# Query products of a row block in pairs of 64-row matmuls, and banks kept free ahead of transposes and products

## The chip, the cores and the metric

One NeuronCore of one Trainium2 chip runs the whole program. The metric is the device time of one execution in microseconds (us). TensorE (PE in the profile) multiplies, VectorE (DVE) reduces and adds, ScalarE (ACT) copies and applies functions, GpSimd (POOL) does small elementwise work and issues some DMAs, SyncE (SP) issues most DMAs. Each engine works through its own queue in order.

## The reference

Two kinds of layer alternate, each with a layer norm ahead and the input added behind: x + A(norm(x)), then x + B(norm(x)), and both once more. x has 2048 rows of 512 float32 values.

```python
def _A_ref(x, dft_seq_re, dft_seq_im, dft_hid_re, dft_hid_im):
    a = jnp.einsum("bsd,ed->bse", x, dft_hid_re)
    b = jnp.einsum("bsd,ed->bse", x, dft_hid_im)
    return jnp.einsum("ts,bse->bte", dft_seq_re, a) - jnp.einsum("ts,bse->bte", dft_seq_im, b)

def _B_ref(x, wq, wk, wv, wo):          # 32 heads of 16, one shared key and value head
    q = (x @ wq).reshape(B, S, 32, 16).transpose(0, 2, 1, 3)
    k, v = x @ wk, x @ wv
    p = softmax(einsum("bhqd,bkd->bhqk", q, k) * 16 ** -0.5)
    o = einsum("bhqk,bkd->bhqd", p, v)
    return o.transpose(0, 2, 1, 3).reshape(B, S, 512) @ wo
```

## The kernel before

The program has two layers; a layer is one A and one B. Float32 products are made of three products of rounded parts (high x high, high x low, low x high), so that `mm3` is three matmuls into one bank of PSUM.

**Phase A** runs over four row blocks `tb` of 512 rows. For each, 32 steps `n` (`n = 32 tb + 16 c + s`) accumulate the sequence transform z over the sixteen 128-row chunks `s`, for the real and the imaginary part `c`, in four banks named x. Up to step 48 the products use all 128 rows. From step 48 on `z_rows` (line 772) issues each as two products of 64 rows, one on the lower half `g = 0` and one on the upper half `g = 1`, into different banks. A group of six such pairs is followed by its counterpart in which the halves have changed banks. Since both halves then write a bank one after the other, `relay` (line 561, ACT copies one column of an operand onto itself) makes the counterpart wait until the first group is finished; another group lies in between. After both parts the y products follow (`y_tile`, or `y_rows` at line 574 on both halves), `y_out` adds the input (line 556), stores the row tile and takes its layer norm statistics (line 141, 142).

**Preparing B** for a row block happens during the next block's steps, from `base = 32 (tb + 1)`, in `prep_tasks`: layer norm (`ln_root`: an addition on DVE at line 147 and a square root on ACT; `ln_inv`: reciprocal on DVE and four operations on POOL; `ln_apply`: DVE, line 189), four transposes (`tr_tile`, line 266, into the one bank z), key and value product (`kv`, a bank y), the difference of key blocks (`k_diff`, line 304), and four query products (`q_mm`, lines 87 to 89 into a bank y, 12 matmuls of 128 rows each) at the ends of the steps `base + 7` to `base + 10`. Each is copied out of PSUM by ACT into the single tile `qraw` (line 82), rounded by ACT into its high part (83), and POOL subtracts for the low part (84). The weights of a query product come from DRAM in two loads (`wq_load`), the result goes to DRAM in six stores (`q_store`), both issued by SP. Block 0 is prepared in the steps 32 to 43, among products of 128 rows; blocks 1 and 2 among products of 64 rows. Block 3 is prepared at the end of the phase in its own way (`q_half`, `q_rows` with 256 columns at line 348, `max_two` at 405).

**Early maxima.** The softmax needs the maximum of each score row. A score product here uses only 64 rows (line 459), so single ones fit between the pairs of phase A; DVE reduces each bank (line 473, or 468 behind a Relu on ACT at 463). `EARLY` lists which query tiles may do so from which step, and by which they must be done. `pump` is called after each pair of products: it takes the entry that is due first, and `issue` picks bank z or the next of the three banks y by a table of estimated times `clk` (`spend` advances it, `held` notes until when a bank is taken). If the bank isn't free by that table nothing is issued. `flush(n)` forces what is due. Inside `q_mm` nothing is pumped.

**Phase B** then computes scores, exponentials and the products with v; the change doesn't touch it.

Lines 79 and 78 are the split of a transform chunk (POOL subtraction and ACT cast), two chunks at the start of every even step; line 759 is the copy of z out of PSUM.

Of the kernel before, what the change touches and what calls it, by code (L numbers as in the profile page):

```python
# [8 lines left out]
F32 = mybir.dt.float32  # L9
# [8 lines left out]
P = 128  # L18
S = 2048
D = 512  # L20
# [27 lines left out]
def fnet_mqa_kernel(ctx: ExitStack, tc: tile.TileContext, x_in, ct, dt_, wq, wkv, wo, out):  # L48
# [48 lines left out]
    nc.gpsimd.memset(v1[:, :, DH:DH + 1], 1.0)  # L97
    kone = sb.tile([P, 1], F32, name="kone")
# [45 lines left out]
    def ln_root(t0, n):  # L144
        v = sb.tile([P, 4], F32, name="lnv", bufs=2)[:, :n]
        w = sb.tile([P, 4], F32, name="lnw", bufs=2)[:, :n]
        nc.vector.tensor_scalar(v, mv[:, t0:t0 + n, 1], EPS, None, op0=ALU.add)
        nc.scalar.activation(w, v, AF.Sqrt)
        return t0, n, v, w
# [44 lines left out]
    def make_layer(L, src, mid, dst, last):  # L194
# [77 lines left out]

        def kv(t0, n, xth, xtl, vt=None, now=True):
            pk = bank("y")[:, :n * P]
            spend(pe=2.9, act=1.2)
            held("y", clk["pe"] + 2.5)
# [39 lines left out]
        def q_mm(tb, g, xth, xtl):  # L316
            wh, wl = st["wqh", g]
            pq = bank("y")
            spend(pe=2.9, act=1.2)
            held("y", clk["act"])  # L320
            for k in range(NK):
                ks = slice(k * P, (k + 1) * P)
                mm3(pq, wh[:, ks], wl[:, ks], xth[:, k, :], xtl[:, k, :], k == 0, k == NK - 1)
            hi = half(4 + 2 * (g % 2), F32R)
            lo = half(5 + 2 * (g % 2), F32R)
            split_act(pq, hi, lo, sb.tile([P, D], F32, name="qraw"))
            st["qs", tb, g] = hi, lo
# [104 lines left out]
        st["skew"], st["rel"], st["subs"] = 0, {}, []  # L432
# [9 lines left out]
        def issue(e, pr, part, g, force):  # L442
            i, kb = EARLY[e][:2]
            tag = "z" if clk["z"] <= clk["y"][0] else "y"
# [5 lines left out]
            if free > clk["pe"] + 0.05 and not force:  # L450
                return False
# [6 lines left out]
            pm = bank(tag)  # L458
            nc.tensor.matmul(pm, o.qT[i][gs, pr, :], k[gs, c0:c0 + 512], start=True, stop=True)  # L459
# [94 lines left out]
        def y_out(t, y, x1):  # L554
            spend(dve=1.3)
            nc.vector.tensor_add(x1, y, x1)  # L556
            nc.gpsimd.dma_start(mid[t], x1)
            ln_stats(x1, t)
# [4 lines left out]
        def y_rows(tb, pairs, zh, zl, x1, after):  # L563
            ys = [pair() for _ in pairs]
            at = 0
            for h in range(2):
                for w, y in zip(pairs, ys):
# [15 lines left out]
                    else:  # L583
                        for e in range(2):
                            y_out(4 * tb + w[e], y[:, e, :], x1[w[e]])
# [71 lines left out]
        def prep_tasks(tb, x1):  # L657
# [3 lines left out]
            def alloc():  # L661
                st["root"] = ln_root(4 * tb, 4)
# [13 lines left out]
            ts[0] = [alloc]  # L676
            ts[1, 1] = [lambda: ln_inv(*st["root"])]
# [7 lines left out]
            ts[6, 3] = [lambda: (kv_lo(4 * tb, 4), k_diff(tb) if tb < 2 else None)]  # L685
            ts[6] = [lambda: v_tr(4 * tb, 4, st["vt"])]
            for g in range(4):
                ts[7 + g] = [lambda g=g: q_mm(tb, g, *st["xt"])]
                if g < 2:
# [528 lines left out]
```

## Time and profile before

| | |
|---|---|
| median of 3 runs | 3548.38 us (3547.25 to 3548.52) |
| the profiled execution | 3548.28 us |
| its span, first to last instruction | 3546.4 us |
| PE busy | 3490.2 us, 98% of the span |
| DVE, ACT, POOL busy | 77%, 70%, 23% |
| chain of work that ended last | PE 93%, DVE 4%, ACT 2% |

In the timeline a row shows start, duration, engine, line, operation, and out<-in by the program's names; in brackets stands how long the engine was idle before it and what released it. Two products of 64 rows that start together stand in one row as x2. A product's duration includes its way through the array, so that neighbours overlap: the distance of two starts shows what a product costs.

### The profile page before, as it was taken

The numbers are of one execution on the slowest core, as the hardware profiler recorded it, in microseconds if no ns is written. First come the engines' busy times: TensorE is split into PE (matmuls) and PEld (weight loads), VectorE is DVE, ScalarE is ACT, GpSimd is POOL, SyncE is SP. The second block draws the span as 40 slices with busy tenths as digits, with TensorE's granted clock in tenths as the row PEclk, the third lists the DMA queues.
The fourth block names the chain that finished last, engine by engine and source line by source line (L and its number), as shares of the span: only waits on it lengthen the run. The fifth ranks groups of instructions, "written<-read, shape, count | busy, mean of one in ns | idle before, by whom it ended". The sixth has DMA issues, their size and how long they took to land.

```text
span 3546.4 us, 64237 instructions
## 1 busy us (share of the span) xinstructions
PE 3490.2 (98%) x24576; PEld 1884.6 (53%) x24576; DVE 2723.9 (77%) x4905; ACT 2499.3 (70%) x3204; POOL 818.7 (23%) x1212
## 2 busy tenths in 40 slices
PE   8999999999999999999999999999999999999999
PEld 6897879433333333333378978783333333333333
DVE  6267776888888888888432777768888888888883
ACT  4223733888888888888932237438888888888888
POOL 4244342211221122112213443322101110111011
PEclk9999999999999999999999999999999999999999
DMA  6445252311111100111144342423111111011100
GB/s 192 148 145 167 82 163 90 85 52 34 35 37 50 35 23 23 50 34 26 40 143 125 125 146 93 149 71 88 46 38 35 49 34 38 23 35 38 37 23 25
DMA packets 224899, 254.54 MB, mean 72 GB/s; under 512 B 52880, under 2 KB 174800, under 8 KB 217424
## 3 DMA queue, kind: packets, MB, share of 16 engines
q1 hardware_dynamic: 210384, 233.12, 21.5%
q0 software_dynamic: 14208, 17.33, 1.6%
q8 instruction: 193, 3.16, 0.4%
q14 instruction: 114, 0.93, 0.1%
HBM read 187.16 MB, written 65.27 MB: 71 GB/s over the span
## 4 chain that ended last, share of the span: by engine, by line
PE 93%; DVE 4%; ACT 2%; issue 1%; POOL 0%; DMA 0%; SPq 0%; ACTq 0%; DVEq 0%; POOLq 0%
PE z L956 29%; PE x L942 19%; PE y L398 13%; PE x L772 11%; PE y L87 3%; PE y L459 3%; PE y L88 2%; PE y L89 2%; PE x L574 2%; PE x L87 2%; PE x L89 2%; PE x L88 2%; DVE mxe L473 1%; DVE mxp L473 1%; PE z L459 1%
## 5 line engine op out<-in xcount | busy, mean ns | idle before, releaser
L945 ACT ACTIVATE slot<-x 128x1024 f32<-128x1024 f32 x2000 | 1946.2, 1024 | 284.2 <-PE x L942 272.3
L399 DVE TENSOR_REDUCE mxp<-y 128x1 f32<-128x512 f32 x2944 | 1849.8, 684 | 179.4 <-PE y L398 167.2
L956 PE MATMUL z<-slot,v 128*32 128x512 f32 x8192 | 1096.3, 605 | 1.6 <-DVE row L960 0.7
L942 PE MATMUL x<-slot,kz 64*128 64x512 f32 x2976 | 677.9, 451 | 0.7 <-DMA slot<-craw 0.4
L942 PEld LDWEIGHTS x<-slot,kz 64*128 64x128 f32 x2976 | 279.3, 184 | 742.9 <-ACT slot L945 686.4
L398 PE MATMUL y<-kz,slot 64*128 64x512 f32 x2176 | 581.2, 396 | 0.7 <-DVE mxp L399 0.4
L956 PEld LDWEIGHTS z<-slot,v 128*32 128x32 f32 x8192 | 163.4, 108 | 362.1 <-issue 331.1
L772 PE MATMUL x<-cl,xnh 64*128 64x512 f32 (+1 forms) x1536 | 352.4, 353 | 0.0
L772 PE MATMUL x<-ch,xnl 64*128 64x512 f32 (+1 forms) x1536 | 347.4, 358 | 1.1 <-ACT xnl L561 1.0
L772 PE MATMUL x<-ch,xnh 64*128 64x512 f32 (+1 forms) x1536 | 339.0, 358 | 6.5 <-DVE row L556 3.9
L398 PEld LDWEIGHTS y<-kz,slot 64*128 64x128 f32 x2176 | 277.5, 186 | 22.6 <-DVE mxp L399 10.4
L79 POOL TENSOR_TENSOR cl<-craw,ch 128x512 fp32r<-128x512 f32 x176 | 225.1, 1299 | 192.3 <-ACT ch L78 180.5
L78 ACT CAST ch<-craw 128x512 fp32r<-128x512 f32 x256 | 153.5, 622 | 156.2 <-PE x L89 81.7
L527 POOL DMA_DIRECT2D slot<-mt x224 | 111.5, 505 | 585.8 <-PE y L398 493.4
L459 PE MATMUL y<-kz,slot 64*128 64x512 f32 x602 | 232.7, 397 | 2.0 <-DVE kraw L304 1.0
L772 PEld LDWEIGHTS x<-ch,xnh 64*128 64x128 f32 x1536 | 210.0, 185 | 24.6 <-issue 6.6
L772 PEld LDWEIGHTS x<-ch,xnl 64*128 64x128 f32 x1536 | 214.3, 185 | 15.8 <-issue 4.5
L772 PEld LDWEIGHTS x<-cl,xnh 64*128 64x128 f32 x1536 | 217.3, 185 | 8.0
L997 POOL TENSOR_TENSOR row<-row,row 128x256 f32<-128x256 f32 x63 | 46.6, 739 | 700.1 <-DMA row<-rd 699.8
L473 DVE TENSOR_REDUCE mxe<-y 128x1 f32<-128x512 f32 x310 | 194.9, 680 | 14.0 <-PE y L459 14.0
L87 PE MATMUL x<-ch,xnh 128*128 128x512 f32 x384 | 154.3, 402 | 10.3 <-ACT ch L78 9.0
L89 PE MATMUL x<-ch,xnl 128*128 128x512 f32 x384 | 153.2, 399 | 2.0 <-POOL xnl L638 1.8
(197 smaller groups left out, 4173.8 us busy)
## 6 DMA issues: line engine op xcount, KB each, us to landing
craw<-ct_in SPq DMA_DIRECT2D x112, 512.0 KB
slot<-qd SPq DMA_DIRECT2D x44, 1024.0 KB
qd<-row SPq DMA_DIRECT2D x144, 128.0 KB
od<-row SPq DMA_DIRECT2D x252, 64.0 KB
row<-wqd SPq DMA_DIRECT2D x48, 256.0 KB
row<-x_in SPq DMA_DIRECT2D x32, 256.0 KB
mid<-row POOLq DMA_DIRECT2D x32, 256.0 KB, 2.4
craw<-ct_in SPq DMA_DIRECT2D x32, 256.0 KB
```

Of the source, the lines that this page charges most:

```text
L78: nc.scalar.copy(hi, raw)
L79: (eng or nc.vector).tensor_sub(lo, raw, f(hi))
L87: nc.tensor.matmul(ps_, ah, bh, start=start, stop=False)
L89: nc.tensor.matmul(ps_, al, bh, start=False, stop=stop)
L398: nc.tensor.matmul(pm, o.qT[i][gs, pr, :], kz[gs, c0:c0 + n], start=True, stop=True)
L399: nc.vector.reduce_max(to, pm, axis=AX.X)
L459: nc.tensor.matmul(pm, o.qT[i][gs, pr, :], k[gs, c0:c0 + 512], start=True, stop=True)
L473: nc.vector.reduce_max(to, pm, axis=AX.X)
L772: nc.tensor.matmul(z[d], a[gs, s, d * P:(d + 1) * P], b[gs, :], start=first and q < 2 and e == 0, stop=last and q > 1 and e == len(turns) - 1)
L942: nc.tensor.matmul(st["e"][:, g, :], kz[64 * g:64 * g + KR, c * P:(c + 1) * P], o.qT[i][64 * g:64 * g + KR, cp:cp + 4, :], start=True, sto ...
L945: nc.scalar.activation(ptiles[i, s_][:, 2 * w:2 * w + 2, :], st.pop("e"), AF.Exp, scale=DH ** -0.5)
L956: nc.tensor.matmul(a[32 * j:32 * j + 32, :], v1[:, c, :], pt[:, j, :], start=c == 0, stop=c == NT - 1)
```

## The change

The query products of a row block are made two at a time in `q_pair`: each of the 24 weight and activation pairings becomes two 64-row matmuls, one on each row half, for two query groups in two banks y; in the second half of the 48 the halves change banks, with a `relay` in between. After every two matmuls `pump` is called. `keep_two` takes the two banks at `(base + 7, 1)` and `(base + 9, 1)`, that is after the second quarter of a step; until the pair is issued only one further use of a bank y is allowed, and bank z. The pairs stand at the ends of the steps `base + 7` and `base + 9`.

`keep` takes a bank y ahead of the key product in the same way. `hold` closes bank z to maxima ahead of each transpose and of the value transposes. The steps of the preparation move forward by up to one step; layer norm goes by two tiles at a time, its addition moves from DVE to POOL, and the square root adds epsilon itself. In `y_rows` both additions come ahead of both statistics. Four of the eight last maxima move from the second `q_rows` to the second half of the first. Starts in `EARLY` move by up to one step.

```diff
-    (1, 0, 2, 44, 49, 63, 16), (2, 0, 3, 44, 49, 63, 16), (3, 0, 8, 45, 49.5, 66, 16), (0, 0, 0, 64, 66.5, 79, 16),
-    (0, 1, 0, None, 71.5, 79, 16), (3, 1, 8, None, 71.5, 84, 16), (4, "f", 2, 77, 79.5, 95, 16), (5, "f", 3, 77, 79.5, 95, 16),
+    (1, 0, 2, 43, 48, 63, 16), (2, 0, 3, 43, 48, 63, 16), (3, 0, 8, 44, 48, 66, 16), (0, 0, 0, 64, 66.5, 79, 16),
+    (0, 1, 0, None, 70.8, 79, 16), (3, 1, 8, None, 70.8, 84, 16), (4, "f", 2, 76, 78.5, 95, 16), (5, "f", 3, 76, 78.5, 95, 16),
...
-        nc.vector.tensor_scalar(v, mv[:, t0:t0 + n, 1], EPS, None, op0=ALU.add)
-        nc.scalar.activation(w, v, AF.Sqrt)
+        nc.scalar.activation(w, mv[:, t0:t0 + n, 1], AF.Sqrt, bias=eps)
+        nc.gpsimd.tensor_scalar(v, mv[:, t0:t0 + n, 1], EPS, None, op0=ALU.add)
...
+        def keep(after):
+            st["pk"], st["kept"] = bank("y"), 3
+            held("y", clk["pe"] + 1.4 + 2.8 + after)
...
+        def keep_two():
+            st["pqs"], st["kept"] = [bank("y"), bank("y")], 2
+            for e in range(2):
+                held("y", clk["pe"] + 1.4 + 5.8 + 0.8 * e)
+
+        def q_pair(tb, g0, xth, xtl, n):
+            pq = st["pqs"]
+            for h in range(2):
+                for k in range(NK)[::1 - 2 * h]:
+                    ks = slice(k * P, (k + 1) * P)
+                    for u in (0, 1, 2)[::1 - 2 * h]:
+                        for g in order(0, 1):
+                            gs = slice(64 * g, 64 * g + 64)
+                            wh, wl = st["wqh", g0 + (g ^ h)]
+                            a, b = ((wh, xth), (wh, xtl), (wl, xth))[u]
+                            nc.tensor.matmul(pq[g ^ h], a[gs, ks], b[gs, k, :],
+                                             start=(h, k, u) == (0, 0, 0), stop=(h, k, u) == (1, 0, 0))
+                        spend(pe=0.231)
+                        pump(n)
+                if h == 0:
+                    relay(xth[:, NK - 1, :1])
+                    pump(n)
+            st["kept"] = 0
+            spend(act=2.4)
+            raw = sb.tile([P, D], F32, name="qraw")
+            for e in range(2):
+                hi, lo = half(4 + 2 * e, F32R), half(5 + 2 * e, F32R)
+                split_act(pq[e], hi, lo, raw if e == 0 else sb.tile([P, D], F32, name="qraw"))
+                st["qs", tb, g0 + e] = hi, lo
...
-            tag = "z" if clk["z"] <= clk["y"][0] else "y"
+            tag = "z" if clk["z"] <= clk["y"][0] and not st["hold"] else "y"
...
+            if tag == "y" and st.get("kept") == 1:
+                return False
...
                         for e in range(2):
-                            y_out(4 * tb + w[e], y[:, e, :], x1[w[e]])
+                            y_add(4 * tb + w[e], y[:, e, :], x1[w[e]])
+                        for e in range(2):
+                            ln_stats(x1[w[e]], 4 * tb + w[e])
...
-            ts[2, 0], ts[2, 2] = [ap(0)], [ap(1)]
-            ts[2] = [lambda: tr(0)]
-            ts[3, 0], ts[3, 2] = [ap(2)], [ap(3)]
-            ts[3] = [lambda: tr(1)]
-            ts[4, 1] = [lambda: tr(2)]
-            ts[4] = [lambda: tr(3), lambda: [wq_load(g) for g in range(2)]]
-            ts[6, 0] = [do_kv]
...
+            ts[0, 0] = [alloc, lambda: root_(0)]
+            ts[0, 2] = [lambda: ln_inv(*roots[0])]
+            ts[1, 1] = [ap(0), lambda: root_(2)]
+            ts[1, 2] = [ap(1), hold]
+            ts[1, 3] = [lambda: ln_inv(*roots[2])]
+            ts[2, 0] = [lambda: tr_(0)]
+            ts[2, 1] = [hold]
+            ts[2, 2] = [ap(2)]
+            ts[2, 3] = [ap(3), lambda: tr_(1)]
+            ts[3, 0] = [hold]
+            ts[3, 1] = [lambda: tr_(2)]
+            ts[3, 2] = [hold]
+            ts[4, 0] = [lambda: tr_(3), lambda: [wq_load(g) for g in range(2)]]
+            ts[4, 3] = [lambda: keep(2.6)]
+            ts[5, 1] = [do_kv]
+            ts[6, 0] = [lambda: (kv_lo(4 * tb, 4), k_diff(tb) if tb < 2 else None), hold]
+            ts[6, 2] = [lambda: (st.update(hold=False), v_tr(4 * tb, 4, st["vt"]))]
+            for e in range(2):
+                ts[7 + 2 * e, 1] = [keep_two]
+                ts[7 + 2 * e] = [lambda e=e: q_pair(tb, 2 * e, *st["xt"], base + 8 + 2 * e)]
+            ts[7].append(lambda: [wq_load(g) for g in (2, 3)])
+            ts[8] = [lambda: [q_store(tb, g) for g in (0, 1)]]
+            ts[10] = [lambda: [q_store(tb, g) for g in (2, 3)]]
...
-            q_rows(14, 0, *xt[1], lambda: None)
+            ticks = iter([0, 0, 0, 0, 1, 1, 1, 1])
+            q_rows(14, 0, *xt[1], lambda: take(mb, next(ticks)))
```

## Rows read from the trace of the kernel before

**Rows 1.** The page, part 2: granted TensorE clock in 40 equal slices, in tenths.

```profile
PEclk9999999999999999999999999999999999999999
```

**Rows 2.** Busy time by stretch: length, then each engine's us (and count).

```profile
136.00:176.00 40.00, 40.00 (x185) 32.35 (x184) 6.38 (x7) 15.48 (x28) 15.78 (x12) 1.00 0.53 157
```

**Rows 3.** Table of waits: who waited for whom, total us, times, longest us.

```profile
PE z L266 <- DVE mxp L473: 7.0, 6, 2.3
PE z L266 <- DVE mxe L473: 5.3, 6, 1.4
PE x L772 <- DVE row L556: 3.9, 4, 1.0
PE y L87 <- DVE mxe L473: 2.8, 6, 0.5
PE y L87 <- DVE mxp L473: 1.9, 4, 0.5
PE y L459 <- DVE kraw L304: 1.0, 2, 0.5
...
ACT lnw L148 <- POOL lnw L157: 11.9, 5, 2.4
```

**Rows 4.** Timeline of PE at three query products of block 1, first layer.

```profile
310.89 0.39 PE L89 MATMUL y<-slot,row 128*128 128x512 f32 x1
311.21 0.51 PE L772 MATMUL x<-ch,xnh 64*128 64x512 f32 x2
311.54 0.39 PE L459 MATMUL y<-kz,slot 64*128 64x512 f32 x1
...
314.79 0.45 PE L772 MATMUL x<-ch,xnl 64*128 64x512 f32 x2
315.17 0.50 PE L87 MATMUL y<-slot,row 128*128 128x512 f32 x1
315.51 0.39 PE L88 MATMUL y<-slot,row 128*128 128x512 f32 x1
...
322.61 0.50 PE L87 MATMUL y<-slot,row 128*128 128x512 f32 x1 [0.46 <-DVE mxp L473]
```

**Rows 5.** Timeline of PE at the turn inside block 3's first query pair.

```profile
621.74 0.28 PE L348 MATMUL x<-xnh,cl 64*128 64x256 f32 x2
622.30 0.38 PE L348 MATMUL x<-xnh,cl 64*128 64x256 f32 x2 [0.28 <-ACT xnh L561]
```

**Rows 6.** Timeline of ACT, then POOL, behind the query product that ends at 311.

```profile
311.31 0.60 ACT L82 ACTIVATE qraw<-y 128x512 f32<-128x512 f32 x1 [5.66 <-PE y L89]
311.94 0.62 ACT L83 CAST row<-qraw 128x512 fp32r<-128x512 f32 x1
312.47 1.14 ACT L78 CAST ch<-craw 128x512 fp32r<-128x512 f32 x2
...
312.72 1.29 POOL L84 TENSOR_TENSOR row<-qraw,row 128x512 fp32r<-128x512 f32 x1 [13.07 <-PE y L459]
```

**Rows 7.** Timeline of PE, then DVE, behind the last y products of block 1.

```profile
270.70 0.50 PE L772 MATMUL x<-ch,xnh 64*128 64x512 f32 x2 [1.01 <-DVE row L556]
...
269.12 0.70 DVE L141 BATCH_NORM_STATS2 bst<-row 128x6 f32<-128x512 f32 x1
```

**Rows 8.** Timeline of POOL and DVE in the layer norm of block 1.

```profile
271.50 2.54 POOL L79 TENSOR_TENSOR cl<-craw,ch 128x512 fp32r<-128x512 f32 x2
271.63 2.45 DVE L147 TENSOR_SCALAR lnv<-mv 128x4 f32<-128x4 f32 x1
```

**Rows 9.** Timeline of PE, then DVE, at the end of the first phase A.

```profile
630.92 0.27 PE L533 MATMUL y<-ident,ms 128*32 128x128 f32 x1 [2.06 <-DVE ms L516]
...
625.16 4.93 DVE L407 TENSOR_REDUCE mxp<-y 128x2 f32<-128x512 f32 x8 [2.86 <-PE y L405]
```

**Rows 10.** Timeline of PE at forced maxima, first layer: first and last row.

```profile
407.97 0.40 PE L459 MATMUL y<-kz,slot 64*128 64x512 f32 x1
...
410.95 0.50 PE L459 MATMUL y<-kz,slot 64*128 64x512 f32 x1 [0.20 <-ACT rel L463]
```

More of the change, by code (lines that the diff above doesn't have):

```diff
@@ L97, in fnet_mqa_kernel @@
     nc.gpsimd.memset(v1[:, :, DH:DH + 1], 1.0)
+    eps = sb.tile([P, 1], F32, name="eps")
+    nc.gpsimd.memset(eps, EPS)
     kone = sb.tile([P, 1], F32, name="kone")
@@ L271, in tr_tile, with kept @@
                 split_ps(v[0], xth, xtl)
+        def keep(after):
+            st["pk"], st["kept"] = bank("y"), 3
+            held("y", clk["pe"] + 1.4 + 2.8 + after)
+        def kept():
+            st["kept"] = 0
+            return st["pk"]
         def kv(t0, n, xth, xtl, vt=None, now=True):
-            pk = bank("y")[:, :n * P]
+            pk = (bank("y") if now else kept())[:, :n * P]
             spend(pe=2.9, act=1.2)
-            held("y", clk["pe"] + 2.5)
+            if now:
+                held("y", clk["pe"] + 2.5)
             for k in range(NK):
@@ L314, in v_tr @@
             nc.scalar.copy(v1[:, t0:t0 + n, :DH], pv_[:, :, DH:])
[L316 to L327, printed above, removed]
+        def keep_two():
[19 more added lines that the diff above has]
+                    pump(n)
+            st["kept"] = 0
+            spend(act=2.4)
[4 more added lines that the diff above has]
+                st["qs", tb, g0 + e] = hi, lo
         def q_half(t0, g, xth, xtl, between=lambda: None):
@@ L431, in make_layer @@
                 for e, ent in enumerate(EARLY)}
-        st["skew"], st["rel"], st["subs"] = 0, {}, []
+        st["skew"], st["rel"], st["subs"], st["hold"] = 0, {}, [], False
+        roots = {}
         def pump(n, only=None):
@@ L458, in issue @@
             pm = bank(tag)
+            if tag == "y" and st.get("kept"):
+                st["kept"] -= 1
+                assert st["kept"]
             nc.tensor.matmul(pm, o.qT[i][gs, pr, :], k[gs, c0:c0 + 512], start=True, stop=True)
@@ L554, in y_out, with y_add @@
         def y_out(t, y, x1):
-            spend(dve=1.3)
+            y_add(t, y, x1)
+            ln_stats(x1, t)
+        def y_add(t, y, x1):
+            spend(dve=1.5)
             nc.vector.tensor_add(x1, y, x1)
             nc.gpsimd.dma_start(mid[t], x1)
-            ln_stats(x1, t)
         def relay(ap):
@@ L661, in alloc @@
             def alloc():
-                st["root"] = ln_root(4 * tb, 4)
                 st["xt"] = [slot(2 + j, F32R).rearrange("p (k t) -> p k t", k=NK) for j in range(2)]
@@ L674, in ap @@
                 return lambda: (spend(dve=0.8), ln_apply(x1[j], x1[j], 4 * tb + j))
-            ts[0] = [alloc]
-            ts[1, 1] = [lambda: ln_inv(*st["root"])]
-            ts[2, 0], ts[2, 2] = [ap(0)], [ap(1)]
-            ts[2] = [lambda: tr(0)]
-            ts[3, 0], ts[3, 2] = [ap(2)], [ap(3)]
-            ts[3] = [lambda: tr(1)]
-            ts[4, 1] = [lambda: tr(2)]
-            ts[4] = [lambda: tr(3), lambda: [wq_load(g) for g in range(2)]]
-            ts[6, 0] = [do_kv]
-            ts[6, 3] = [lambda: (kv_lo(4 * tb, 4), k_diff(tb) if tb < 2 else None)]
@@ L686, in prep_tasks, with hold, tr_ @@
[L686 to L689, printed above, removed]
-                    ts[7 + g].append(lambda g=g: wq_load(g + 2))
-                if g:
-                    ts[7 + g].append(lambda g=g: q_store(tb, g - 1))
-            ts[11] = [lambda: q_store(tb, 3)]
+            def hold():
+                st["hold"] = True
+            def tr_(tt):
+                st["hold"] = False
+                tr(tt)
@@ new lines, in root_ @@
+            def root_(e):
+                roots[e] = ln_root(4 * tb + e, 2)
+            ts[0, 0] = [alloc, lambda: root_(0)]
[8 more added lines that the diff above has]
+            ts[3, 0] = [hold]
```

4 rows, old and new, of the table EARLY are left out of this document.

## The prediction, made before the changed kernel ran

> **What bounds the kernel now.** The profiled execution took 3548.28 us around a span of 3546.4 us; that is 0.1 us from the median of the three runs, so a change of the span is taken as a change of the time. The page comes first: TensorE (PE) is busy nearly throughout, and its clock is granted in full (2.4 GHz) in every slice [rows 1]. So nothing is gained off PE, and a microsecond counts only if PE's stream of products gets shorter or loses a gap. "Busy" hides small gaps, because products overlap: two 64-row products, one on each row half, start together and last 0.39 us, while the next two start 0.23 us later. The second view is therefore PE's own table of waits, which says where its stream stands still and for whom [rows 3]; the third is the timeline of single stretches, read by the distance of starts against that pitch of 0.23 us. The phases with the sequence transform (about 0 to 632 and 1772 to 2394 us) hold everything that the change touches. In them the preparation of row block 0 runs among 128-row products: 136 to 176 us are 40.00 us busy of 40.00 [rows 2], there is nothing to gain there. Blocks 1 and 2 are prepared among 64-row products with single row maxima ("maxima" below: one 64-row product of 512 columns, then a DVE reduction that frees its bank) between them, and there the waits lie.
>
> **What the change takes away** (both layers together, four preparations of blocks 1 and 2):
>
> *Turns between 64 and 128 rows.* Each of the 16 query products is a run of 12 full products among 64-row ones. Going in, the starts lie 0.38 us apart instead of 0.23 (0.15 lost), going out 0.32 and then 0.33 (0.09 and 0.10) [rows 4]; the second pitch inside is 0.34 (0.11). That is 0.45 us a product, 16 x 0.45 = 7.2 us. As pairs of 64-row products they take the same pitch as their neighbours, and this goes. The Trainium skill says so too (TensorEngine Tiling (Array Packing), Key Properties: changing the tiling mode, not just the tile, drains the engine); by it alone the turn would go as well, so the sum is the same.
>
> *Waits of query products for a bank.* 2.8 + 1.9 us in ten waits [rows 3], such as 0.46 us at 322.61 [rows 4]. With two banks set aside half a step ahead they go: 4.7 us, and 0.07 us each for refilling the pipe, 5.4 us.
>
> *Waits of transposes.* 7.0 + 5.3 us in twelve waits [rows 3]: the one z bank is held by a maximum whose reduction stands in DVE's queue. Closing z ahead of each transpose takes that away. But the transposes now come up to three quarters of a step earlier (a step is 2.8 us of products), and the first of a block then waits for its normalised rows. That chain stands behind two subtractions on POOL, 2.54 us together, in POOL's queue ahead of the new addition [rows 8]; they start when the y additions are out, some 0.7 us earlier than now. By my estimate its end and the due time of the transpose fall together, with no slack. In return DVE loses an operation that took 2.45 us beside POOL's subtractions, for 4 columns [rows 8]. I take 10.5 us of the 12.3; bounds 6 and 12.3.
>
> *The y additions first.* After the last y products PE waits for the addition that frees its bank, 3.9 us in four waits [rows 3], 270.70 one of them; the statistics that now go behind (0.70 us, and a short aggregate) stood between the two additions [rows 7]. 3.3 us.
>
> *The wait for the K difference.* 1.0 us in two waits [rows 3], with refilling and the maxima behind it about 2.8; the bank is now counted as taken 2.6 us longer and the subtraction starts half a step earlier. I take half, 1.4; bounds 0 and 2.8.
>
> *End of the phase.* PE waits 2.06 us for the last maxima, whose eight reductions run from 625.16 for 4.93 us, 0.616 each [rows 9]. Four of them may start behind the first query pair, about 2 us earlier. The last then ends near 628.0 instead of 630.1, about when PE has finished its products, so nearly the whole wait goes: 1.8 us a layer, 3.6.
>
> *Maxima forced at their due time.* Between 407.97 and 410.95 eight single products start and nothing else, where 0.12 us each would do: 2.0 us a layer [rows 10]. The pairs now let about five maxima through where a query product let none, and starts move up by up to a step, so fewer are left. I take 2.5 us of 4.0; bounds 0 and 4.0.
>
> Together 12.6 + 10.5 + 3.3 + 1.4 + 3.6 + 2.5 = **33.9 us**.
>
> **What the change adds.**
>
> *A turn inside each pair.* Both row halves write both banks, so the second half of a pair starts only when the first half is finished and ACT has copied one column onto itself. The same sequence stands at the end of the phase with 256 columns: starts 621.74 and 622.30, 0.56 us where 0.12 (half of 0.23) would do, 0.44 lost [rows 5]. The 128-row form needs no such turn. A single maximum (0.12) may fill part of it: 0.35 us, eight pairs, 2.8 us; bounds 1.6 and 3.6. The Trainium skill speaks against the change here (TensorEngine Tiling (Array Packing), Gotcha 1: different row tiles cannot access the same PSUM bank simultaneously); it gives no price, so the sum stays with the row.
>
> *Behind each pair: ACT and POOL.* This is the term that decides. A query product leaves ACT two copies, 0.60 and 0.62 us, the first starting 0.42 us after the start of its last product (310.89), then POOL a subtraction of 1.29 us from 312.72 [rows 4, 6]. Until now the next came a step and a product later. Now two results are finished at once, and both go through the one tile `qraw`. The second copy out of PSUM has to wait until POOL has read the first. That a copy waits for POOL to release a reused tile is in the trace (ACT's Sqrt behind POOL, 11.9 us in five waits) [rows 3]. Counted from the start of the pair's last product: first bank free at 1.02, second copy of it to 1.67, POOL 1.83 to 3.12, second bank free at 3.8, last copy to 4.45. The planner counts them free 7.2 and 8.0 us after they are set aside, and itself counts 6.9 us of products and some 0.7 of maxima from there to the pair's end. So it sends the next maximum into the first bank at 0.47 (PE waits to 1.07: 0.6) and, one or two pitches later, another into the second bank at 1.85 (PE waits to 3.85: 2.0). PE's queue is in order, so the transform's products stand behind that. 2.6 us a pair, eight pairs: 20.8 us. Were no maximum to go there, PE would still need ACT's one-column copy of the next step, behind two casts of 0.57 us [rows 6]: ready about 5.9, needed about 3.7, 2.2 us. Bounds: 0.6 a pair (4.8), if the second copy doesn't wait, and 3.2 (25.6).
>
> *Block 0.* Its products run without a gap [rows 2]; two pairs a layer now put a turn in and out (0.45) and one inside (0.44) there, with no maxima to fill it: 4 x 0.89 = 3.6 us. Behind the second pair POOL reaches the low part of a transform chunk only after both query subtractions, at about 7.2, and PE needs it at 6.2: 1.0 us a layer. 5.6 us; bounds 2 and 7.
>
> Weights: the second pair's four loads (1 MB) start behind the first pair with two steps and its stalls to land, 8 us and more; counted at nothing, and 1 us a pair if that cover falls short. The stores on SP are the same in number; they wait for the same copies.
>
> Together 2.8 + 20.8 + 5.6 = **29.2 us**. Net 4.7 us shorter: 3548.3 - 4.7 = **3543.6 us**. The time is a small difference of two large terms.
>
> **Rivals.**
>
> *The copies behind a pair cost little.* If the maxima find other banks until the second copy is out, or `qraw` isn't waited for, 0.6 us a pair stays: 16 us less, 3527.6, own range 3519 to 3536. For it: z and the third bank are free then, and PE's waits named in the table are short. Against it: the planner's own figures make both banks free at once.
>
> *The transposes wait for POOL instead of DVE; slower.* The new addition and the normalising chain stand on POOL behind two subtractions of 1.27 us [rows 8], with no slack by the sum above. If they come 2 us later, each block's first transpose waits over 2 us again, the scaling holds up DVE's reductions behind it, and so the next transposes: the 10.5 us are lost and about 1.5 us a block added. 3543.6 + 10.5 + 6 = 3560. It decides from a delay of about 2 us on. Against it: the additions come earlier, and the chunk subtractions may start earlier with them.
>
> *The halves don't run together.* A pair needs two weight loads. If they went one after the other, the pitch would be near 0.37 and each pair 3.4 us longer, 12 pairs, 3584 us. The Trainium skill has loads cost by their columns, not by their rows (TensorE: Matmul & The Clock Gate, LDWEIGHTS), which alone would ask for that. The neighbours in the same form keep 0.23, so this has hardly a chance.
>
> **How the numbers follow.** Forecast 0.48 (own range 3537 to 3551), cheap copies 0.33, POOL slower 0.17, halves 0.02. A measurement of this kernel tells about 0.2%, 7 us, from no change. Faster by more (under 3541.3): all of the second case and a quarter of the forecast, 0.45. Slower by more: most of the third and the last, 0.16. Within: 0.39. The range 3524 to 3553 takes in the second case's centre and the forecast with its bounds; it leaves out the third case and the far end of the second.
>
> **What would show it.** Right: no gap ahead of transposes in blocks 1 and 2 beyond the turn's 0.2 us; query pairs at a pitch of 0.23 with one gap near 0.45 in the middle; behind each pair ACT's second copy starting at the end of POOL's subtraction, with PE waiting for it near 2 us. Wrong: PE running on behind a pair (second case), or transposes waiting for the scaling behind POOL (third).

## The result, and the profile after

The changed kernel takes 3555.13 us in the median (3551.99 to 3558.51), the kernel before 3550.38 (3547.25 to 3552.29): a ratio of 1.0014, 95% interval 1.0008 to 1.002. It is 4.75 us slower where 4.7 us were to be gained, and lies above the range. The profiled execution has a span of 3552.1 us, 5.7 more than before's.

The table shows where the 5.7 us arise. It takes the start of each step's transform products in both timelines, less the pitch of the products between them; what is left is how far one kernel falls behind the other, step by step. Each timeline is one execution, with the clock falls of that one.

| part of the change | forecast, us | measured, us |
|---|---|---|
| y additions first | -3.3 | -4.2 |
| transposes | -10.5 | -8.8 |
| **K difference: steps of the key product and the value transposes** | **-1.4** | **+8.5** |
| query products of blocks 1 and 2 (-12.6 + 2.8 + 20.8) | +11.0 | +8.1 |
| block 0 | +5.6 | +5.3 |
| end of the phase | -3.6 | -2.8 |
| forced maxima | -2.5 | -0.9 |
| the rest | 0 | +0.5 |
| sum | -4.7 | +5.7 |

PE's table of waits in the changed kernel (waiting engine, tile and line <- releaser: us in total, times, longest) answers [rows 3]:

```profile
PE y L493 <- ACT qraw L82: 6.7, 8, 1.2
PE z L268 <- DVE row L191: 3.5, 3, 2.2
PE y L342 <- ACT slot L598: 3.4, 12, 0.3
PE y L493 <- DVE kraw L315: 2.5, 2, 1.3
PE x L88 <- POOL cl L79: 1.5, 2, 0.8
PE y L493 <- DVE kz L305: 1.1, 2, 0.6
```

The twelve waits of transposes for reductions and the four for y additions are gone. In their place stand eight waits for `qraw`, one for each pair of blocks 1 and 2; twelve turns inside pairs; one long wait of a transpose, now for the scaled row (the other two of the three stood before as well, at block 3); two late chunks in block 0; and the wait for the K difference, which was 1.0 us and is now 2.5, with 1.1 for the subtraction ahead of it.

**The K difference.** The timelines of DVE and PE in the changed kernel, block 1 of the first layer (start, us, engine, line, operation, out <- in, count, [idle before <- releaser]):

```profile
300.27 0.69 DVE L507 TENSOR_REDUCE mxp<-y 128x1 f32<-128x512 f32 x1 [0.26 <-PE x L825]
301.00 1.39 DVE L305 TENSOR_TENSOR kz<-y,kz 16x512 fp32r<-16x512 f32 x2
302.40 0.69 DVE L315 TENSOR_TENSOR kraw<-kraw,y 128x512 f32<-128x512 f32 x1
...
303.24 0.46 PE L493 MATMUL y<-kz,slot 64*128 64x512 f32 x1 [1.27 <-DVE kraw L315]
```

A single maximum has been sent into the bank of the key product, and waits until DVE has read it. DVE does that in 0.69 us, but first it reduces a fourth maximum (300.27) and makes the two subtractions of `kz`. Before, three maxima stood ahead of them and PE waited 0.50 us. What follows costs more than the wait. PE's busy time and granted clock by stretch, in the changed kernel and then in the kernel before (stretch, its length, busy (count), granted clock, DMA share, GB/s):

```profile
305.00:306.00 1.00, 1.00 (x8) 0.67 0.00 0
306.00:307.00 1.00, 1.00 (x8) 0.50 0.00 0
307.00:308.00 1.00, 1.00 (x8) 0.50 0.00 0
308.00:309.00 1.00, 1.00 (x8) 0.63 0.00 0
...
2067.00:2069.00 2.00, 2.00 (x11) 0.50 0.00 0
```

```profile
305.00:306.00 1.00, 0.74 (x5) 1.00 0.00 0
306.00:307.00 1.00, 1.00 (x12) 1.00 0.00 0
```

Behind the wait TensorE's clock falls from 2.4 to 1.2 GHz. The four stretches of 1 us hold 0.66 + 1 + 1 + 0.74 = 3.4 us at half clock with PE busy throughout: 1.7 us lost. In the second layer it is twice that, 6.8 us and 3.4 lost. Waits of 3.6 us instead of 1.0 and 5.1 us of half clock make 7.7 of the 8.5; the rest is put down to the refilling of the pipe and was not measured apart. PE shows as 1.00 busy in all of it; the clock column tells, and the count beside it (8 products started in a microsecond instead of 12). The page's row of clocks is all nines here as in [rows 1], since a slice of 89 us hides such a stretch.

**Behind a query pair.** ACT, POOL and PE in the changed kernel, first pair of block 1:

```profile
317.10 0.60 ACT L82 ACTIVATE qraw<-y 128x512 f32<-128x512 f32 x1 [3.39 <-PE y L342]
319.81 0.60 ACT L82 ACTIVATE qraw<-y 128x512 f32<-128x512 f32 x1 [1.46 <-POOL row L84]
...
318.51 1.27 POOL L84 TENSOR_TENSOR row<-qraw,row 128x512 fp32r<-128x512 f32 x1 [15.38 <-PE x L825]
...
313.76 1.45 PE L342 MATMUL y<-slot,row 64*128 64x512 f32 x10 [0.28 <-ACT slot L598]
320.46 0.49 PE L493 MATMUL y<-kz,slot 64*128 64x512 f32 x1 [1.18 <-ACT qraw L82]
```

This is as forecast, down to the place: the second copy starts at 319.81, when POOL's subtraction ends (318.51 + 1.27 = 319.78), and a maximum in the second bank holds PE until it is out. PE stands still for 1.18 us there, not 2.0. The turn inside the pair is the 0.28 at 313.76, 0.45 to 0.52 us by the distance of starts.

**The end of the phase.** DVE's last reductions and PE's outer products behind them, changed kernel:

```profile
627.57 4.92 DVE L435 TENSOR_REDUCE mxp<-y 128x2 f32<-128x512 f32 x8 [0.89 <-PE y L433]
...
633.34 0.27 PE L567 MATMUL y<-ident,ms 128*32 128x128 f32 x1
634.82 0.50 PE L426 MATMUL y<-kz,slot 64*128 64x512 f32 x1 [0.78 <-DVE mxp L427]
```

The eight reductions start 0.89 us behind DVE's last work instead of 2.86, and the wait of 2.06 us of [rows 9] is gone; 0.78 us of it comes back at the next maxima.

**The forced maxima.** They are forced at two places. PE at the first of them, changed kernel, first and last row:

```profile
413.04 0.50 PE L493 MATMUL z<-kz,slot 64*128 64x512 f32 x1
...
416.58 0.49 PE L493 MATMUL y<-kz,slot 64*128 64x512 f32 x1 [0.19 <-ACT rel L497]
```

From 413.04 up to 416.58 nine single products start and nothing else, in 3.54 us, where [rows 10] has eight in 2.98 us. Here none has gone. The second place, which [rows 10] does not show, is the next due time; in the kernel before, first and last row:

```profile
554.10 0.40 PE L459 MATMUL y<-kz,slot 64*128 64x512 f32 x1
...
555.29 0.50 PE L459 MATMUL y<-kz,slot 64*128 64x512 f32 x1 [0.18 <-DVE mxe L468]
```

Five single products start there and nothing else, in 1.19 us (and at 2316.06 in the second layer). In the changed kernel no such row of maxima is left at that place, and the two steps around it are 1.35 and 1.15 us shorter in the two layers. The first place costs 1.6 us more than before, the second 2.5 less.

### The profile page after: what moved, and what is told of

It is laid out like the page before. It is cut to its first block, busy times and chain, and to the rows that moved or that the text cites. A ratio compares the mean times of both kernels' runs of the same rounds, so it can differ in the third digit from the quotient of the medians.

```text
span 3552.1 us, 64858 instructions
## 1 busy us (share of the span) xinstructions
PE 3502.6 (99%) x24864; PEld 1872.6 (53%) x24864; DVE 2720.8 (77%) x4892; ACT 2504.3 (71%) x3222; POOL 830.9 (23%) x1262
## 5 line engine op out<-in xcount | busy, mean ns | idle before, releaser
L426 PE MATMUL y<-kz,slot 64*128 64x512 f32 x2176 | 581.8, 396 | 1.9 <-DVE mxp L427 1.9
L825 PE MATMUL x<-ch,xnh 64*128 64x512 f32 (+1 forms) x1536 | 347.7, 359 | 2.3 <-ACT row L812 2.2
L493 PE MATMUL y<-kz,slot 64*128 64x512 f32 x622 | 247.5, 405 | 12.2 <-ACT qraw L82 6.7
L825 PEld LDWEIGHTS x<-ch,xnl 64*128 64x128 f32 x1536 | 205.8, 185 | 18.7 <-ACT xnl L598 3.8
```

The costliest lines, as they stand in the source:

```text
L426: nc.tensor.matmul(pm, o.qT[i][gs, pr, :], kz[gs, c0:c0 + n], start=True, stop=True)
L825: nc.tensor.matmul(z[d], a[gs, s, d * P:(d + 1) * P], b[gs, :], start=first and q < 2 and e == 0, stop=last and q > 1 and e == len(turns) - 1)
```

## Experiments

Times are medians; each ratio is to the kernel before, run on the same chip (3550.5 to 3550.9 us). "Changed kernel" is the kernel after, 3555.1. A profile is one execution of several, and where its clock falls differs between executions; readings by steps come from that one.

**1. The second copy of a pair in a tile of its own.** Everything else as in the changed kernel.

```
-            raw = sb.tile([P, D], F32, name="qraw")
...
-                split_act(pq[e], hi, lo, raw if e == 0 else sb.tile([P, D], F32, name="qraw"))
+                split_act(pq[e], hi, lo, f(lo))
```

> The changed kernel, but the second copy out of PSUM no longer shares the tile qraw: ACT copies each result into the tile of its low part, and POOL subtracts there in place. Theory (ACT waits for POOL behind each pair, and PE for ACT): in the profile ACT's second copy starts right behind its first cast instead of 2.7 us after the first copy; PE's waits for ACT's copies behind pairs (6.7 us in eight in the changed kernel) fall to under 2, and the time by 5 to 8 us against the changed kernel, to about that of the kernel before. Rival (the maxima in between hide it, PE's waits only move to the next bank): under 2 us.

Measured: 3545.66 us, ratio 0.9985 (0.9976 to 0.9994), 9.5 below the changed kernel. ACT in this run, behind the same pair:

```profile
318.42 0.60 ACT L82 ACTIVATE row<-y 128x512 f32<-128x512 f32 x1 [3.37 <-PE y L342]
...
319.58 0.59 ACT L82 ACTIVATE row<-y 128x512 f32<-128x512 f32 x1
```

The second copy starts 1.16 us behind the first, instead of 2.71, and waits for nothing; the eight waits for `qraw` are out of PE's table. Step by step each pair of blocks 1 and 2 is 1.05 to 1.52 us shorter, 10.3 together, and the late chunk of block 0 goes too (about 1.9 us). So the one tile `qraw` is the cause of the waits behind pairs, and 10.3 us its price in blocks 1 and 2. Clock falls at other places (285.7 and 415.4 us are two) take some of it back.

**2. Single 128-row query products again,** in all blocks and at their old steps, with the rest of the change kept (the first maxima of block 0 then start at their old times too).

```
-            for e in range(2):
-                ts[7 + 2 * e, 1] = [keep_two]
-                ts[7 + 2 * e] = [lambda e=e: q_pair(tb, 2 * e, *st["xt"], base + 8 + 2 * e)]
+            for g in range(4):
+                ts[7 + g] = [lambda g=g: q_mm(tb, g, *st["xt"])]
...
```

> The changed kernel with the four query products of 128 rows of before in all blocks, at the old steps; all else as changed. Counted along the steps of the two profiles, pairs cost about 2 us more than single products in each of the blocks 1 and 2 (8 us) and 2.6 us in block 0 (5 us). Theory: 11 to 14 us faster than the changed kernel, 6 to 9 us faster than before. Rival (the losses stand in the steps of the key product and not in the pairs): 4 us or less from the changed kernel.

Measured: 3543.24 us, ratio 0.9982 (0.9973 to 0.9991), 11.9 below the changed kernel. The query steps of blocks 1 and 2 are 10.8 us shorter, block 0 4.5. Part of it comes back: 3.1 us at the first forced maxima, with clock falls, and 3.7 at the end of the phase, where the second row of forced maxima stands again. In blocks 1 and 2 that is what the pairs reach too once their copies don't wait (10.3). A pair saves the turns between 64 and 128 rows, and loses about as much by its own turn in the middle (0.45 to 0.52 us) and by the maximum that meets its first bank (0.2 to 0.4).

**3. Single query products in block 0 alone.** The same edit under `if tb == 0`.

> The changed kernel with the single query products of before in block 0 alone. Theory (two turns of row mode, two turns inside and one late chunk in each layer): 5 us faster than the changed kernel, half of it in each layer, all between the steps 39 and 46. Rival (block 0 has cover): nothing.

Measured: 3549.66 us, ratio 0.9999 (0.999 to 1.0008), 5.5 below the changed kernel, against the 5.6 us of the sum and the 5.3 of the traces.

**4. The bank of the key product counted as taken 2 us longer.**

```
-            ts[4, 3] = [lambda: keep(2.6)]
+            ts[4, 3] = [lambda: keep(4.6)]
```

> The changed kernel with one number changed: the planner counts the bank of the key product as taken 2.0 us longer (4.6 instead of 2.6). No maximum is then sent between the key product and the value transposes into that bank. Theory (PE's wait of 1.3 us for the key difference in block 1, and the clock at 1.2 GHz behind it for 3.4 and 6.8 us): both are gone from block 1, in both layers, and the time falls by 5 to 8 us. Rival A (the clock falls there without the wait): the stretches near 305 and 2064 us stay, and 2 to 3 us are gained. Rival B (the maxima held back wait elsewhere): under 1 us.

Measured: 3549.19 us, ratio 0.9997 (0.9988 to 1.0006), 5.9 below the changed kernel. PE's stretches in this run:

```profile
305.00:306.00 1.00, 0.98 (x8) 1.00 0.86 262
306.00:307.00 1.00, 0.85 (x8) 1.00 0.01 0
307.00:308.00 1.00, 1.00 (x9) 1.00 0.00 0
```

No maximum meets the bank, the wait for `kraw` is out of the table, and the clock stays at 2.4 GHz where it fell. So the changed kernel counted the bank free too early. In this profile the steps of the K difference are 6.1 us shorter than in the changed kernel, of the 8.5; some comes back as a wait of the transform for the copy of the values (1.8 us in two). The profile is of the longest of the eleven executions, 3555.48 us: its clock falls for 3.4 us at five other places between the products, behind transposes, query pairs and forced maxima (286.3 and 416.0 us are two), where the profile of the changed kernel has none. How many such falls the median execution has is not on record.

**5. The same wait, put into the kernel before.** Two additions of 0.69 us on DVE, whose results are overwritten, ahead of the K difference of block 1.

```
             t = st["kraw"]
+            for _ in range(2):
+                nc.vector.tensor_add(kd, t, t)
```

> The kernel before with two more DVE additions of 512 columns (0.69 us each, into a tile that is written over afterwards) ahead of the key difference of block 1. It doubles one wait of before. Theory (a wait long enough lets the clock fall): PE's wait for the key difference grows from 0.5 to near 1.9 us, a stretch at half clock follows within some microseconds in one layer or both, and the time grows by 1.4 us a layer for the wait and 1.7 or 3.4 us a layer for the clock: 5 to 9 us. Rival (only the wait counts): 2 to 3 us, the clock stays full.

Measured: 3555.99 us, ratio 1.0015 (1.0006 to 1.0024), 5.5 above the kernel before. PE's wait and PE's stretches in this run:

```profile
306.24 0.50 PE L461 MATMUL y<-kz,slot 64*128 64x512 f32 x1 [1.96 <-DVE kraw L306]
...
307.00:308.00 1.00, 0.77 (x6) 0.91 0.00 0
308.00:309.00 1.00, 1.00 (x6) 0.50 0.00 0
309.00:310.00 1.00, 1.00 (x8) 0.50 0.00 0
```

The wait grows from 0.50 to 1.96 us, and the clock falls behind it, with nothing of the change in the kernel. Step by step each layer loses 2.7 us there, for a wait that is 1.4 us longer. In the second layer the clock falls behind the same wait (1.96 us at 2071.30, fall at 2072.51). All eleven executions took longer than any of the kernel before, so this is not one unlucky profile. That a wait of this kind brings the clock down here is thereby shown; that every such wait does is not (see the last section).

**6. Key product, K difference and value transposes at their old steps,** no bank set aside for them, and the start times of the maxima of the keys as before (71.5 and 103.5 instead of 70.8 and 102.8).

```
-            if now:
-                held("y", clk["pe"] + 2.5)
+            held("y", clk["pe"] + 2.5)
...
-            ts[4, 3] = [lambda: keep(2.6)]
-            ts[5, 1] = [do_kv]
-            ts[6, 0] = [lambda: (kv_lo(4 * tb, 4), k_diff(tb) if tb < 2 else None), hold]
-            ts[6, 2] = [lambda: (st.update(hold=False), v_tr(4 * tb, 4, st["vt"]))]
+            ts[6, 0] = [do_kv]
+            ts[6, 3] = [lambda: (kv_lo(4 * tb, 4), k_diff(tb) if tb < 2 else None)]
+            ts[6] = [lambda: v_tr(4 * tb, 4, st["vt"])]
...
```

> The changed kernel with the key product, the key difference and the value transposes at the steps of before, no bank set aside for them and z open to maxima there. Theory (in the changed kernel PE waits 1.3 us for the bank of the key difference, and TensorE's clock falls to 1.2 GHz for 3.4 and 6.8 us behind that wait): the wait falls to 0.5 us, no stretch at half clock is left in block 1, and the time falls by 6 to 9 us. Rival A (the move itself costs, not the clock): full clock only changes 0 to 2 us. Rival B (the clock falls whatever stands there): the half-clock stretches stay, at other places.

Measured: 3563.16 us, ratio 1.0037 (1.0024 to 1.0049), 8.0 above the changed kernel. PE's table of waits in this run has new lines:

```profile
PE z L492 <- ACT v L324: 4.2, 2, 2.1
PE z L268 <- DVE mxp L506: 3.8, 2, 1.9
```

The K steps of block 1 are 1.85 and 3.0 us shorter, and the clock no longer falls there in the first layer; in the second it falls for 3.4 us instead of 6.8, behind a new wait of 2.10 us (2075.15, for the copy of the values). A wait as long, for the same copy, stands in the first layer (309.29) and leaves the clock as it is. The maxima, moved with them, now meet the value transposes and block 3. The undo moved more than the suspect and decides nothing about it; experiments 4 and 5 do.

**7. Another form of the scaling.** Rows of blocks 0 to 2 scaled by `scalar_tensor_tensor` instead of `tensor_scalar`.

> The changed kernel, with the scaling of the normalised rows in blocks 0 to 2 as a two-tensor operation on DVE (the factor broadcast along the row) instead of a tensor-scalar operation. Theory (a tensor-scalar operation on DVE stands still while POOL runs its subtractions: 4.12 us at 281.5 beside 5.0 us of POOL): all these scalings take near 0.7 us, the wait of 2.2 us of the third transpose in block 1 goes, and the time falls by 2 to 5 us. Rival (the operation waits for its operands, the row shows the wait): its duration stays near 4 us, the time the same.

Measured: 3558.71 us, ratio 1.0024 (1.0014 to 1.0033), 3.6 above the changed kernel. The third scaling of block 1 on DVE, and POOL beside it:

```profile
282.75 4.59 DVE L715 SCALAR_TENSOR_TENSOR row<-row,mv,rs 128x512 f32<-128x512 f32 x1
287.86 0.74 DVE L715 SCALAR_TENSOR_TENSOR row<-row,mv,rs 128x512 f32<-128x512 f32 x1
...
281.81 2.54 POOL L79 TENSOR_TENSOR cl<-craw,ch 128x512 fp32r<-128x512 f32 x2
284.30 2.48 POOL L84 TENSOR_TENSOR slot<-row,slot 128x512 fp32r<-128x512 f32 x2
```

The other form stands still here beside POOL just as the first does (4.12 us in the changed kernel), and costs 0.74 instead of 0.53 where it is free.

**8. The scaling ahead of POOL.** The third and fourth scaling issued behind the first transpose.

```
-            ts[2, 0] = [lambda: tr_(0)]
+            ts[2, 0] = [lambda: tr_(0), ap(2), ap(3)]
```

> The changed kernel, with the third and fourth scaling of rows in blocks 0 to 2 (tensor_scalar on VectorE) issued three quarters of a step earlier, behind the first transpose. Theory: in the changed kernel the third scaling of block 1 takes 4.12 us at 281.51 instead of 0.5, because it starts while GpSimd runs its four subtractions of 280.37 to 285.34, and ends with them; the third transpose waits 2.19 us for it. Its mean and root are there at 279.25, ahead of GpSimd's subtractions and of VectorE's reductions. Issued there it takes 0.5 us a piece, the table's waits of transposes for scaled rows (3.5 us in three) go, and the time falls by 3.5 to 5 us, to 3550 to 3552. Rival: the operation waits for its rows or their root and not for GpSimd; then the waits stay within 1 us of 3.5 in sum, or go to the second transpose, and the time stays at 3555.

Measured: 3562.88 us, ratio 1.0042 (1.0028 to 1.0057), 7.8 above the changed kernel. DVE, POOL, and PE's table in this run:

```profile
280.08 0.55 DVE L191 TENSOR_SCALAR row<-row,mv,rs 128x512 f32<-128x512 f32 x1 [1.15 <-POOL rs L160]
280.54 4.73 DVE L191 TENSOR_SCALAR row<-row,mv,rs 128x512 f32<-128x512 f32 x1
...
281.26 2.50 POOL L79 TENSOR_TENSOR cl<-craw,ch 128x512 fp32r<-128x512 f32 x2
283.72 1.25 POOL L84 TENSOR_TENSOR slot<-row,slot 128x512 fp32r<-128x512 f32 x1
...
PE y L493 <- DVE mxp L507: 5.8, 2, 4.0
```

The root came out at 280.05, as POOL's last step ahead of its subtractions. One scaling passed in 0.55 us; the next was caught and ended at 285.27, 0.30 behind POOL's three subtractions. It had begun 0.72 us before the first of them (281.26), while POOL was issuing transfers (280.06, for 1.19 us). Four reductions now stood behind it, and PE waited 4.0 us for one of them. The remedy failed, and it shows that not one scaling's place in the program makes it slow: now another one is, beside the same row of subtractions.

**9. Two parts of the change alone,** in the kernel before: the y additions ahead of the statistics, and four of the last eight maxima taken behind the first pair.

> The kernel before with two parts of the change alone: the y additions ahead of the statistics, and four of the last eight maxima of the phase taken behind the first pair of its last query products. Theory (the parts add up as the step by step comparison of the two traces has them): -4.15 us for the additions and -3.6 to -5.3 for the end of the phase, 3550.5 - 7.8 to 9.5 = 3541 to 3543. Rival: the gain at the end comes from the changed spread of maxima over the blocks and not from the four taken early; then only the additions are left, 3546.

Measured: 3544.81 us, ratio 0.9983 (0.9974 to 0.9993), 6.1 below the kernel before, between the two theories. The trace has the parts as they were in the whole: 3.9 us for the additions, and the wait for the last maxima 2.0 us a layer shorter. What takes some of it back is the clock behind a transpose of block 1: it waits 2.26 us for its bank at 279.97, as it did before at 280.92 with the clock at 1.00, and now the clock falls behind it (at 280.60 and 2041.88; 1.6 us in each layer by the steps). Two waits of 0.8 us at block 3 are new. The transpose in this run:

```profile
279.97 0.66 PE L266 MATMUL z<-ident,row 128*128 128x128 f32 x4 [2.26 <-DVE mxp L473]
```

**10. The mended parts together.** The copy of its own, the bank taken 2 us longer and single products in block 0; first with the other scaling of experiment 7, then without it, then with the scaling of experiment 8.

> The changed kernel with four edits together: single query products in block 0, the low part's tile in place of qraw in the pairs, the longer count for the key product's bank, the scaling as a two-tensor operation. If the gains add up (9.5 and 5 us as measured one by one, 5 to 8 and 2 to 5 as expected for the other two): 20 to 25 us faster than the changed kernel, 16 to 20 us faster than before. If the clock falls at other places instead, half of that.

Measured: 3536.93 us, ratio 0.9959 (0.9947 to 0.9972).

> The changed kernel with three edits: the bank of the key product counted as taken 2.0 us longer, the second copy of a query pair into the tile of its own low part, and block 0 with single 128-row query products. It is the best version so far without the other form of the scaling, which by itself cost 3.6 us. Theory that the parts add up: 3555.1 - 5.9 - 9.5 - 5.5 = 3534.2, some 3533 to 3537 (the in-place copy is worth less where block 0 has no pairs). Rival: the clock falls to 1.2 GHz at other waits as one is taken away, 3537 to 3541.

Measured: 3531.24 us, ratio **0.9948** (0.9934 to 0.9963), 19.7 below the kernel before and 23.9 below the changed one. PE's stretches in this run:

```profile
271.00:300.00 29.00, 26.73 (x203) 1.00 0.48 158
300.00:400.00 100.00, 98.13 (x820) 1.00 0.51 156
400.00:620.00 220.00, 216.37 (x2092) 1.00 0.35 110
2000.00:2365.00 365.00, 359.47 (x3234) 1.00 0.37 117
```

The parts add up and 3 us more: 5.9 + 9.5 + 5.5 = 20.9. The clock stays at 2.4 GHz from 271 to 620 and from 2000 to 2365 us; it falls only at the ends of the phases, as in the kernel before. The run with the other form of the scaling is 5.7 us longer. That this is the form's own price is not shown: its profile has four clock falls of 3.4 us that this one lacks (19.5, 285.7, 412.0 and 2166.5 us), 6.8 us together.

> The version before this one with the third and fourth scaling issued earlier, behind the first transpose. Theory: 3.5 to 5 us less than it, about 3530. Rival, as for the scaling alone: no change.

Measured: 3539.45 us, ratio 0.9971 (0.9961 to 0.9982): 8.2 us above the kernel without the earlier scaling, with a wait of 4.1 us and two clock falls in its profile (281.5 and 2039.4 us).

## Why the prediction was wrong

**The step that failed is "the wait for the K difference".** The text took half of 2.8 us as a gain, because the bank "is now counted as taken 2.6 us longer and the subtraction starts half a step earlier", and set the lower bound at nothing. It measured 8.5 us the other way, which is 9.9 of the 10.4 us between forecast and profile.

The ground of the gain was not there. The kernel before, too, counted the bank as taken behind the product: `kv` advances the planner's time by its product and then calls `held("y", clk["pe"] + 2.5)`. `keep(2.6)` adds 1.4 for the half step up to the product, 2.8 for the product, and 2.6. Counted from the end of the product, the planner takes the bank as occupied for 2.6 us instead of 2.5: 0.1 us longer, not 2.6. Nor does an earlier subtraction help, since the product moves with it: three quarters of a step lie between the two in both kernels. So nothing in the change could shorten the wait. Experiment 4 gives the bank the 2 us that the text thought it had, and the wait goes.

Two things made it longer. What stands ahead of the subtraction on DVE was not counted in the new order: a fourth reduction besides the subtractions of `kz`, so that the bank comes free at 303.09 (302.40 + 0.69), 5.65 us after the key product's last product has ended (297.05 + 0.39), against 4.70 before. And no row of a stretch behind a wait was read for its clock. The waits cost 2.6 us more than before, the clock 5.1 us. Experiment 4 takes both away, experiment 5 makes both in the kernel before.

**Forced maxima** came out at -0.9 for -2.5, inside the bounds, but not where the text looked. At the place of [rows 10] it lost 1.6 us: 302 maxima have started ahead of that step; before, 304 had. The 2.5 us came at the next due time, which the text didn't count: by then 533 have started, and before 527. That part is due to the pairs, as forecast: in experiment 1, which has them, the second row of forced maxima is gone, and in experiments 2 and 9, with single products, it stands. Experiment 2 has the moved starts of the changed kernel, so these alone don't take it away. That the sum of the two falls inside the bounds is luck.

**Behind each pair** the mechanism was right in each link (one `qraw`, ACT held by POOL, a maximum in the second bank holding PE), and experiment 1 shows it by taking the tile away. The size was not: 10.3 us for the second copies, where 2.0 us of each 2.6 were to be theirs, 16 us. In the pair shown, the maximum that met the second bank stood waiting from 319.28, 2.2 us behind the start of the first copy, where the text had it at 1.4 (1.85 less 0.42). The query steps as a whole came out at +8.1 instead of +11.0.

**Transposes:** 8.8 us of the forecast 10.5, inside the bounds. In blocks 1 and 2 the waits for reductions went altogether. One long wait is left, for the third scaling of block 1 in the first layer:

```profile
279.71 1.89 DVE L507 TENSOR_REDUCE mxp<-y 128x1 f32<-128x512 f32 x3 [1.58 <-PE y L493]
281.51 4.12 DVE L191 TENSOR_SCALAR row<-row,mv,rs 128x512 f32<-128x512 f32 x1
286.16 0.53 DVE L191 TENSOR_SCALAR row<-row,mv,rs 128x512 f32<-128x512 f32 x1
...
280.37 2.54 POOL L79 TENSOR_TENSOR cl<-craw,ch 128x512 fp32r<-128x512 f32 x2
...
285.78 0.63 PE L268 MATMUL z<-ident,row 128*128 128x128 f32 x4 [2.19 <-DVE row L191]
```

So the second rival had its place right, POOL's subtractions beside the normalising, and its reason half: not POOL's own chain is late, but one of DVE's scalings stands still beside POOL. [Rows 8] had shown the like, an operation on 4 columns that took 2.45 us beside the same subtractions; the sum used it as a gain and not as a price for what stands there next. In the second layer the same scaling passed in 0.54 us (last section).

**The rest held.** y additions -4.2 for -3.3, block 0 +5.3 for +5.6 (experiment 3: 5.5, with the late chunk as forecast, 0.76 us of wait at 181.14), the turn inside a pair 0.45 to 0.52 us for 0.35, and the end of the phase -2.8 for -3.6. There the reductions start 2.0 us earlier, as forecast, the wait of 2.06 us goes and 0.78 comes back; the clock behind it in the first layer was low for 6.8 us and not for 10.2. The rival of cheap copies did not come: the second copy waits in each of the eight pairs. Its 16 us were 9.5 us of time when experiment 1 made the copies cheap.

The net was a small difference of two large terms, and the text says so; yet its range allowed 9 us upwards, and the one term of the K difference, whose lower bound was set at nothing, came out 9.9 us above its forecast. The other terms are off by less than 3 us each and together by 0.5.

## What to carry to other kernels

Before a reservation is priced as longer than the one it replaces, both are counted from the same event: here 2.6 us were 0.1. And the account of when a PSUM bank comes free goes through the queue of the engine that reads it, in the new order; a maximum sent 1.3 us too soon stops every product behind it. Two results finished at once want two staging tiles: one tile shared by ACT and POOL puts POOL's time between them. Where an engine is always busy, a wait is priced with the clock of the stretch behind it, read in windows of a microsecond.

## What the runs showed of the hardware that was not expected

**TensorE's clock falls in the middle of a busy phase.** After waits of 1.27 us (303.24) and 1.96 us (experiment 5) it was granted at 1.2 instead of 2.4 GHz for 3.4 us, 2.1 and 1.6 us after the wait had ended, while PE was busy; in the second layer of the changed kernel for 6.8 us. Not every wait does it. The wait of 2.19 us at 285.78 left the clock at 1.00 in the profile of the changed kernel; the same wait, of 2.20 and 2.19 us, brought it down as it ended in experiments 1 and 4. The wait of 2.26 us of a transpose left it at 1.00 in the kernel before and brought it down in experiment 9. What decides it stays open.

**DVE's scaling can stand still beside POOL's subtractions,** in both forms: 4.12, 4.59 and 4.73 us instead of 0.53 to 0.74, each ending 0.3 to 0.6 us behind POOL's last subtraction in a row. That was once in each of these profiles, at block 1 of the first layer. In the second layer of the changed kernel the same scaling passed between the subtractions of POOL:

```profile
2046.97 0.54 DVE L191 TENSOR_SCALAR row<-row,mv,rs 128x512 f32<-128x512 f32 x1
```

POOL subtracts there from 2044.65 on, and its next two subtractions start at 2047.14. Others beside POOL in blocks 1 and 2 took 0.92 to 1.63 us, and the pair that experiment 8 moved took 1.49 us each in its second layer (2051.88 and 2053.29). Reductions out of PSUM do not stand still: those of 279.71 take 0.63 us each while POOL subtracts from 280.37 on. The Trainium skill has a rule for it (SBUF — State Buffer, SBUF: two separate sides): VectorE, when its operation runs in a two-port mode or has two inputs in SBUF, and GpSimd share one pair of SBUF ports, which whichever starts first holds for its whole instruction. The three long scalings agree with a lock of this kind in that they end behind POOL, and go further, since they did not get in between three or four subtractions that followed each other on POOL; the one of 0.54 us did. The scaling of experiment 8 began before the first of the subtractions and was held all the same. What decides stays open, and so does whether these scalings run in a two-port mode.
